# A chunked retention and gated-MLP kernel: one stretch of small products per chunk, a shorter weight conversion, another order

## The chip, the cores and the metric

The kernel runs on one core of a Trainium2 chip. TensorE (PE) multiplies into PSUM, with its weight loads shown apart (PEld); VectorE (DVE), ScalarE (ACT) and GpSimd (POOL) work on vectors; SyncE (SP) issues loads. The metric is the device time of one execution in microseconds (us), the median of several runs; smaller is better. The profile is one profiled execution, whose span runs from its first to its last instruction.

## The reference

Eight heads of linear attention with a decay, then a gate from a causal convolution of five taps, and two products with 512x512 weights. B = 4, S = 768, 8 heads of 64; the weights and taps come as float64.

```
gamma = 1.0 - 2.0 ** (-5.0 - np.arange(H))
for t in range(S):
    state = gamma * state + outer(k[:, :, t], v[:, :, t])
    y[:, :, t] = scale * (q[:, :, t] @ state)
x = y.transpose(0, 2, 1, 3).reshape(B, S, H * D)
gate = sigmoid(sum(conv_w[k] * xp[:, k:k + S] for k in range(5)))
out = (gate * (x @ w_val)) @ w_out
```

## The kernel before

The sequence is cut in 24 chunks of 128 tokens (g = 0 to 23), six per batch entry; chunks 4n to 4n+3 are the same tokens of the four entries and make unit n. A chunk's q, k, v (1 MB, tile `att`) come with one load on SP, five chunks deep. GpSimd multiplies v by its decay (`decay`, L251).

A chunk's attention is a series of small products, 64x64 in float32, each a quarter of the TensorE array; an fp32 product is two instructions in the profile. In each half of 64 tokens: `scores` (q times k, L261) into the left half of the tile `sy`; VectorE masks them into `u` (`mask`, L271); `y_scores` (u times v, L299) into the right half of `sy`; `state` adds k times v to the running state `z_ps` in PSUM (L283); ScalarE copies the state before each half (`snap`, L294); `y_state` adds that state times q (L299). VectorE scales y into `x` (`evac`, L344). On TensorE this is two blocks a chunk: `block_a` has y_scores and the first half's state, `block_b` the second half's state, y_state and, from chunk 6 on, the next chunk's scores. `block_b` comes after ScalarE's snapshot, with big products between the blocks.

A unit's MLP: for each of four column blocks m, `conv` (first tap on ScalarE, four on VectorE, L445, of which the planner may put two on TensorE, `pe_tap`, L454) and the sigmoid; `x` is split in a rounded part `xh` (ScalarE, L353) and a rest `xl` (GpSimd, L357); a value tile is 12 big products (`val`, L471), with which VectorE multiplies the gate (`gated`, L480); the result is split too (L487, L491). An output tile is 12 products (`outp`, L499) over all four blocks, copied by ScalarE (L509) and sent (L513). 24 value and 24 output tiles are 576 big products.

The float64 weights come as pairs of 32-bit words (`wst`) in eight tiles of 128x512. For each, VectorE runs five instructions (L388, L394, L400, L404, L417), ScalarE one (L409), GpSimd the sum (L413); then the split in two parts (L428, L432).

The order on every engine is written out by `plan`: each piece of work is a `Step` with a due time, an engine, a cost and the tiles that it reads and writes; the planner takes the step that can start first by its costs, the earliest due among equals. Due times stand in the constants at L534 to L543. An engine works strictly in that order.

Of the kernel before, what the change touches and what calls it, by code (L numbers as in the profile page):

```python
# [21 lines left out]
EARLY = 6  # L22
LB = 5
WB = 4
XB = 4
XS = 6
GV = 6
LATENCY, LANDING = 0.15, 1.8
PAGE, FETCH, CROWDED = 128, 3.4, 5.0
TINY = 2.0 ** -15 * (1.0 + 1.0 / 8.0)  # L30
LO, HI = slice(0, HALF), slice(HALF, P)

# [8 lines left out]
class Step:  # L41
    def __init__(self, due, engine, cost, reads, writes, fn, args):
        self.due, self.engine, self.cost, self.fn, self.args = due, engine, cost, fn, args
        self.reads, self.writes = reads, writes
        self.waits, self.then = set(), []
        self.next = []
        self.after = []
        self.lag = 0.0
        self.ready = 0.0
        self.words = 0  # L50
        self.other = None


def plan(steps):
# [31 lines left out]
    for ring in rings.values():  # L86
        for i, (k, s) in enumerate(ring):
            if i >= k.bufs:
                for b in users[ring[i - k.bufs][0]]:
                    wait(s, b)  # L90
            if i and s not in ring[i - 1][1].next:
                s.waits.add(ring[i - 1][1].index)
                ring[i - 1][1].next.append(s)
    clock, free = {}, {}
# [10 lines left out]
    order, words, paged = [], PAGE - 28, [0.0, 0.0]  # L105
    while any(free.values()):
        start, _, e = min(
            (max(clock[e], min(s.ready for s in f)), e, e) for e, f in free.items() if f
        )
        s = min((s for s in free[e] if s.ready <= start), key=lambda s: (s.engine != e, s.index))  # L110
        free[s.engine].remove(s)
        if s.other:
            free[s.other[0]].remove(s)
            if s.engine != e:
                s.engine, s.cost, s.fn = s.other
        order.append(s)
        clock[e] = start + s.cost
        if e == "PE" and s.words:

            left, now = s.words, start  # L120
            while left >= words:
                now += s.cost * words / s.words
                left -= words
                paged.append(now)
                slow = clock.get("DMA", 0.0) > now
                now, words = max(now, paged[-2] + (CROWDED if slow else FETCH)), PAGE
            words -= left
            clock[e] = max(clock[e], now + s.cost * left / s.words)
        for t in s.next:
            t.ready = max(t.ready, start)  # L130
            if t not in s.then:
                t.waits.discard(s.index)
                if not t.waits:
                    offer(t)
        for t in s.then:
            late = LANDING if e == "DMA" else 0.0 if t.engine == e else LATENCY
            t.ready = max(t.ready, clock[e] + late + s.lag)
            t.waits.discard(s.index)
            if not t.waits:
                offer(t)  # L140
    assert len(order) == len(steps)
# [4 lines left out]
def tile_retention_gated_mlp(  # L146
# [7 lines left out]
    eye: bass.AP,  # L154
    out: bass.AP,
):

# [13 lines left out]
    stage = ctx.enter_context(tc.tile_pool(name="stage", bufs=2))  # L194
    ps_y = ctx.enter_context(tc.tile_pool(name="ps_y", bufs=1, space=PSUM))
    ps_s = ctx.enter_context(tc.tile_pool(name="ps_s", bufs=1, space=PSUM))
# [3 lines left out]

    small_sb = const.tile([P, small.shape[1]], F32, name="small_sb")
    vd_sb = small_sb[:, 0:48].rearrange("p (c x) -> p c x", x=8)
    ra_sb = small_sb[:, 48:72].rearrange("p (c x) -> p c x", x=4)
    tri_sb = small_sb[:, 72:136]
    pos_sb = const.tile([2, P + 512], F32, name="pos_sb")
    cw_sb = const.tile([P, NPAIR, TAPS], F32, name="cw_sb")
    eye_sb = const.tile([P, P], F32, name="eye_sb")
    diag = const.tile([P, NPAIR, 2, P], F32, name="diag")
# [13 lines left out]
    def at(due, engine, cost, reads, writes, fn, *args):  # L222
        steps.append(Step(due, engine, cost, list(reads), list(writes), fn, args))

    parts, gates, gparts, xbufs = {}, {}, {}, {}
    chunks = [(b, c) for c in range(NCH) for b in range(B)]

# [17 lines left out]
    def sy_of(g):  # L245
        return sy1 if g < EARLY and g % 2 else sy0

# [6 lines left out]

    def scores(g):
        sy = sy_of(g)
        q, kT = halves(g, 0), halves(g, 1)
        for j in range(2):
            for s in range(2):
                for x, rows, cols in ((0, LO, LO), (1, HI, LO), (1, LO, HI), (0, HI, HI)):  # L260
# [6 lines left out]

    def mask(g):
        sy = sy_of(g)
        us[g] = mlp.tile([P, 2, 4, HALF], F32, name="u")  # L270
# [5 lines left out]
        )  # L276

# [13 lines left out]
    def snap(g, s):  # L291
        b, c = chunks[g]
        sn = mlp.tile([P, 2, 2, HALF], F32, name="snap", bufs=3)
# [3 lines left out]
    def y_mm(g, h, cols, j, s, lhsT, rhs, start):  # L297
        off = 256 + (2 * j + s) * HALF
        nc.tensor.matmul(  # L299
            sy_of(g)[cols, h, off:off + HALF], lhsT=lhsT, rhs=rhs,  # L300
# [9 lines left out]

    def y_state(g):
        b, c = chunks[g]
        q = halves(g, 0)
        for s in (1, 0):
            if c == 0 and s == 0:
                continue
# [4 lines left out]

    def first_pos():
        pos_ps.append(sy1[:, 0])
# [18 lines left out]
    def evac(g):  # L342
        b, c = chunks[g]
        nc.vector.tensor_tensor(  # L344
            xs[c][:, :, b, HALO:].rearrange("p (h j) t -> p h j t", h=2),
            sy_of(g)[:, :, 256:512].rearrange("p h (j t) -> p h j t", t=P),
# [4 lines left out]
    def round_x(n, ct):  # L351
        xh[n, ct] = mlp.tile([P, B, P], F32R, name="xh", bufs=XS)
        nc.scalar.copy(xh[n, ct], xs[n][:, ct, :, HALO:])  # L353

    def rest_x(n, ct):
        xl[n, ct] = mlp.tile([P, B, P], F32R, name="xl", bufs=XS)
        nc.gpsimd.tensor_tensor(  # L357
            xl[n, ct], xs[n][:, ct, :, HALO:], xh[n, ct].bitcast(F32), op=ALU.subtract
        )


    raws = {}

    def load_w(n):
        st = stage.tile([P, 512, 2], I32, name="wst", bufs=WB)
        src = w64[n // 4, n % 4].bitcast(I32).rearrange("p (n two) -> p n two", two=2)
        nc.sync.dma_start(out=st, in_=src)
        raws[n] = st

    cvt = {}  # L370

    def words(n):
        raw = raws[n]
        lo16 = raw.rearrange("p n two -> p (n two)").bitcast(U16).rearrange(
            "p (n four) -> p n four", four=4
        )[:, :, 1]
        return raw[:, :, 1], lo16

    def cv_bits(n):
        hi, _ = words(n)  # L380
        size = hi.shape[1]
        bits = ps_a.tile([P, 512], I32, name="acc")[:, 0:size]
        cvt[n] = (
            bits,
            stage.tile([P, size], I32, name="top"),
            stage.tile([P, size], F32, name="rest"),
        )
        nc.vector.tensor_scalar(  # L388
            bits, hi, 3, 0x3FFFFFFF, op0=ALU.logical_shift_left, op1=ALU.bitwise_and
        )  # L390

    def cv_top(n):
        bits, top, _ = cvt[n]
        nc.vector.scalar_tensor_tensor(  # L394
            top, words(n)[0], -0x40000000, bits, op0=ALU.bitwise_and, op1=ALU.bitwise_or
        )

    def cv_exp(n):
        bits, top, _ = cvt[n]
        nc.vector.tensor_scalar(bits, top, -0x800000, None, op0=ALU.bitwise_and)  # L400

    def cv_rest(n):
        bits, _, rest = cvt[n]
        nc.vector.scalar_tensor_tensor(  # L404
            rest, words(n)[1], 2.0 ** -36, bits.bitcast(F32), op0=ALU.mult, op1=ALU.mult
        )

    def cv_size(n):
        nc.scalar.activation(cvt[n][0].bitcast(F32), words(n)[0].bitcast(F32), AF.Abs)  # L409

    def cv_sum(n):
        _, top, rest = cvt[n]
        nc.gpsimd.tensor_tensor(rest, rest, top.bitcast(F32), op=ALU.add)  # L413

    def cv_flush(n):
        bits, _, rest = cvt[n]
        nc.vector.scalar_tensor_tensor(  # L417
            cw_sb.rearrange("p a k -> p (a k)") if n == "cw" else rest,
            bits.bitcast(F32), TINY, rest, op0=ALU.is_ge, op1=ALU.mult,
# [7 lines left out]
    def cv_round(n):  # L427
        nc.scalar.copy(parts_of(n)[0], cvt[n][2])  # L428

    def cv_low(n):  # L430
        h, l = parts_of(n)
        nc.gpsimd.tensor_tensor(l, cvt[n][2], h.bitcast(F32), op=ALU.subtract)  # L432
# [17 lines left out]
    def make_diag(m, i):  # L450
        nc.scalar.mul(diag[:, m, i], eye_sb, cw_sb[:, m, 1 + i:2 + i])

    def pe_tap(n, m, k):
        nc.tensor.matmul(  # L454
            accs[n, m], lhsT=diag[:, m, k - 1], rhs=xs[n][:, m, :, k:k + P],
            start=False, stop=True, skip_group_check=True,
        )

# [4 lines left out]
    def val(n, m, i):  # L463
# [3 lines left out]
        if i == 0:  # L467
# [6 lines left out]
            rhs=xx[n, ct].rearrange("p b t -> p (b t)"),  # L474
# [14 lines left out]
    def rest_gv(n, m):  # L489
        gvh, gvl = gvs[n, m]  # L490
        nc.gpsimd.tensor_tensor(gvl, gate.pop((n, m)), gvh.bitcast(F32), op=ALU.subtract)  # L491
# [23 lines left out]

    warm = nc.const_aps.tensor(0.0, (P, 1), F32).bitcast(BF16)[:, 0:1]

    def warm_up(i):

        dst = ps_a.tile([P, 512], F32, name="acc") if i < 2 else sy1[:, i % 2]  # L520
        nc.tensor.matmul(  # L521
            dst, lhsT=warm.broadcast_to([P, P]), rhs=warm.broadcast_to([P, 512]),
# [11 lines left out]
    MM = 0.232  # L534
    EARLY_AT = 3.46
    EARLY_STEP = 2.26
    LATE_AT = 29.71
    LATE_STEP = 6.0
    MLP_AT = 31.96
    MLP_STEP = 3.6  # L540
    SPLIT_LEAD = 5.44
    CONV_LEAD = 6.16
    W_AT = (9.3, 13.0, 15.6, 22.7, 36.8, 32.1, 37.6, 38.1)  # L543
# [3 lines left out]
    def load_at(due, g):  # L547
        loaded[g] = due
        a = [("att", g % LB, "qk"), ("att", g % LB, "vk")]
        if g == 0:  # L550
            at(due, "DMA", 3.2, [], a[0:1], load, g, slice(0, 2))
            at(due, "DMA", 1.6, [], a[1:2], load, g, slice(2, 4))
            at(due, "ACT", 0.4, [], ["small"], get, small_sb, small)
            at(due, "ACT", 0.4, [], ["pos"], get, pos_sb, pos)
# [277 lines left out]
```

## Time and profile before

| what | value |
|---|---|
| runs | 229.59, 229.29, 228.21 us; median 229.29 us |
| span of the profiled execution | 226.3 us (the page gives no other time for it) |
| busy: PE, DVE, ACT, POOL | 208.8, 140.0, 106.7, 105.9 us |

The page's slices show TensorE's share, the granted clock and the transfers in 40 equal parts of 5.66 us, in tenths:

```profile
PE   8666796797999999999999999999999999999993
DVE  0499858999999959377376329973339752911000
PEclk9857559999999999999999999999999999999999
DMA  6999979855145634564446524010111111111122
```

For ten slices the transfers are at their limit, VectorE fills up and TensorE has gaps; from the eleventh on TensorE is full to the end. Lines in the prediction have an engine, a line number and a tile, as in `PE mm L471`: a big product of a value tile.

### The profile page before, as it was taken

What the parts mean: (1) busy time and instruction counts of PE and PEld (TensorE: products, weight loads), DVE (VectorE), ACT (ScalarE), POOL (GpSimd) and SP (SyncE); (2) the same over time, 40 slices, a digit from 0 to 9 for tenths busy, and PEclk for the clock granted to TensorE, in tenths of its full rate; (3) what the DMA queues carried; (4) which work ended last, traced back from release to release, by engine and by line L of the source; (5) the groups of instructions that cost most, each with busy time, mean ns of one, the idle gap of its engine ahead of it and who ended that gap; (6) DMA issues with size and microseconds to landing.
All of it is one profiled execution on the core that took longest, in us unless ns stands there. A gap on an engine that the chain in (4) does not pass through costs nothing.

```text
span 226.3 us, 7941 instructions
## 1 busy us (share of the span) xinstructions
PE 208.8 (92%) x3551; PEld 162.8 (72%) x3551; DVE 140.0 (62%) x212; ACT 106.7 (47%) x218; POOL 105.9 (47%) x93
## 2 busy tenths in 40 slices
PE   8666796797999999999999999999999999999993
PEld 3365684665876787787777787777777888788883
DVE  0499858999999959377376329973339752911000
ACT  2373375455858346652472364541456437331421
POOL 0267889466999316824451644600526217220400
PEclk9857559999999999999999999999999999999999
DMA  6999979855145634564446524010111111111122
GB/s 205 421 414 416 410 271 363 305 212 184 30 167 191 211 123 181 185 226 133 151 197 234 186 77 175 38 49 5 47 49 46 46 46 49 46 46 46 46 93 96
DMA packets 8822, 36.32 MB, mean 161 GB/s; under 512 B 1106, under 2 KB 1618, under 8 KB 5844
## 3 DMA queue, kind: packets, MB, share of 16 engines
q1 hardware_dynamic: 4752, 29.36, 34.6%
q10 hardware_dynamic: 4036, 6.45, 7.6%
q8 instruction: 28, 0.46, 0.8%
q14 instruction: 6, 0.05, 0.1%
HBM read 29.52 MB, written 6.29 MB: 158 GB/s over the span
## 4 chain that ended last, share of the span: by engine, by line
PE 80%; DVE 10%; issue 4%; DMA 2%; POOL 1%; ACT 1%; ACTq 0%; POOLq 0%
PE mm L499 28%; PE mm L471 27%; PE sy L299 10%; PE z_ps L283 5%; PE sy L261 5%; PE sy L521 2%; DVE acc L445 2%; DMA out_dram<-o_sb 2%; DVE acc L400 1%; DVE x L344 1%; DVE rest L417 1%; DVE top L394 1%; POOL rest L413 1%; DVE u L271 1%; PE acc L454 1%
## 5 line engine op out<-in xcount | busy, mean ns | idle before, releaser
L445 DVE SCALAR_TENSOR_TENSOR acc<-x,cw_sb,acc 128x512 f32<-128x512 f32 x94 | 70.2, 753 | 19.3 <-ACT acc L443 17.4
L357 POOL TENSOR_TENSOR xl<-x,xh 128x512 fp32r<-128x512 f32 x24 | 30.5, 1293 | 39.8 <-PE mm L471 24.8
L491 POOL TENSOR_TENSOR gvl<-gate,gvh 128x512 fp32r<-128x512 f32 x24 | 30.8, 1294 | 28.4 <-ACT gvh L487 18.4
L499 PE MATMUL mm<-woh,gvl 128*128 128x512 f32 (+1 forms) x100 | 39.2, 392 | 0.0
L499 PE MATMUL mm<-wol,gvh 128*128 128x512 f32 (+1 forms) x100 | 39.2, 392 | 0.0
L499 PE MATMUL mm<-woh,gvh 128*128 128x512 f32 (+1 forms) x100 | 39.2, 392 | 0.0
L251 POOL TENSOR_TENSOR att<-att,small_sb 128x512 f32<-128x512 f32 x24 | 25.0, 1045 | 29.4 <-DMA att<-in_att_dram 29.3
L480 DVE TENSOR_TENSOR gate<-mm,gate 128x512 f32<-128x512 f32 x24 | 16.4, 687 | 22.5 <-PE mm L471 22.5
L509 ACT COPY o_sb<-mm 128x512 f32<-128x512 f32 (+1 forms) x25 | 14.2, 569 | 31.8 <-PE mm L499 30.2
L471 PE MATMUL mm<-xh,wvh 128*128 128x512 f32 x96 | 27.8, 406 | 0.1
L471 PE MATMUL mm<-xl,wvh 128*128 128x512 f32 x96 | 27.8, 402 | 0.0
L471 PE MATMUL mm<-xh,wvl 128*128 128x512 f32 x96 | 27.4, 400 | 0.0
L283 PE MATMUL z_ps<-att 64*64 64x64 f32 x704 | 22.2, 242 | 3.5 <-ACT snap L294 2.7
L299 PEld LDWEIGHTS sy<-u,att 64*64 64x64 f32 x768 | 16.1, 154 | 12.9 <-issue 6.8
L283 PEld LDWEIGHTS z_ps<-att 64*64 64x64 f32 x704 | 17.2, 151 | 10.2 <-ACT snap L294 6.2
L299 PE MATMUL sy<-u,att 64*64 64x64 f32 x768 | 19.2, 244 | 5.0 <-DVE u L271 3.1
L487 ACT CAST gvh<-gate 128x512 fp32r<-128x512 f32 x24 | 14.9, 620 | 18.3 <-PE mm L499 9.3
L461 ACT ACTIVATE gate<-acc 128x512 f32<-128x512 f32 x24 | 14.3, 596 | 18.7 <-POOL gvl L491 10.8
L344 DVE TENSOR_TENSOR x<-sy,dec 128x512 f32<-128x512 f32 x20 | 13.8, 689 | 14.8 <-PE sy L261 14.2
L294 ACT COPY snap<-z_ps 128x256 f32<-128x256 f32 x44 | 15.2, 372 | 15.7 <-PE z_ps L283 15.3
L499 PEld LDWEIGHTS mm<-wol,gvh 128*128 128x128 f32 x100 | 18.8, 188 | 4.1
L499 PEld LDWEIGHTS mm<-woh,gvh 128*128 128x128 f32 x100 | 18.8, 188 | 4.1
(46 smaller groups left out, 269.9 us busy)
## 6 DMA issues: line engine op xcount, KB each, us to landing
att<-in_att_dram SPq DMA_DIRECT2D x23, 1024.0 KB, 6.9
out_dram<-o_sb ACTq DMA_DIRECT2D x23, 256.0 KB, 2.0
wst<-in_w_dram SPq DMA_DIRECT2D x8, 512.0 KB, 7.4
att<-in_att_dram SPq DMA_DIRECT2D x2, 512.0 KB, 4.8
out_dram<-o_sb ACTq DMA_DIRECT2D x2, 128.0 KB, 1.9
small_sb<-in_small_dram ACTq DMA_DIRECT2D x1, 68.0 KB, 4.5
eye_sb<-in_eye_dram ACTq DMA_DIRECT2D x1, 64.0 KB, 9.2
cw_raw<-in_conv_w_dram ACTq DMA_DIRECT2D x1, 20.0 KB, 7.0
```

What stands on the lines that cost most here:

```text
L251: nc.gpsimd.tensor_tensor(v, v, vd_sb[:, c, :].unsqueeze(2).broadcast_to([P, 8, HALF]), op=ALU.mult)
L283: nc.tensor.matmul(z_ps[cols, x, b, j], lhsT=k[rows, x, j, s, :], rhs=v[rows, x, j, s, :], start=g == 0 and s == 0 and j == 0, stop=True, ...
L294: nc.scalar.copy(sn, z_ps[:, :, b])
L299: nc.tensor.matmul(sy_of(g)[cols, h, off:off + HALF], lhsT=lhsT, rhs=rhs, start=start, stop=True, skip_group_check=True,)
L344: nc.vector.tensor_tensor(xs[c][:, :, b, HALO:].rearrange("p (h j) t -> p h j t", h=2), sy_of(g)[:, :, 256:512].rearrange("p h (j t) -> p ...
L357: nc.gpsimd.tensor_tensor(xl[n, ct], xs[n][:, ct, :, HALO:], xh[n, ct].bitcast(F32), op=ALU.subtract)
L445: nc.vector.scalar_tensor_tensor(acc, x[:, :, k:k + P], cw_sb[:, m, k:k + 1], acc, op0=ALU.mult, op1=ALU.add,)
L471: nc.tensor.matmul(vps[n, m], lhsT=w[:, m, ct * P:(ct + 1) * P], rhs=xx[n, ct].rearrange("p b t -> p (b t)"), start=(i == 0), stop=(i == 3 ...
L480: nc.vector.tensor_tensor(gv, vps.pop((n, m)), gv, op=ALU.mult)
L487: nc.scalar.copy(gvs[n, m][0], gate[n, m])
L491: nc.gpsimd.tensor_tensor(gvl, gate.pop((n, m)), gvh.bitcast(F32), op=ALU.subtract)
L499: nc.tensor.matmul(ops[n, b, cs.start][:, 0:cs.stop - cs.start], lhsT=gg[:, b * P:(b + 1) * P], rhs=w[:, ct, cs], start=(i == 0), stop=(i ...
```

## The change

The small products. A chunk from 4 on has one stretch: `visit` (y_scores of g, second state half of g, first state half of g+1), then, in the planner held directly behind it, `rest_of_visit` (y_state of g, scores of g+1). Between them stands `turn`, a ScalarE copy of one column of `sy` on 64 partitions, which waits for products of `visit`, and for which those of `rest_of_visit` wait. The first four chunks read no state: their scores are taken over the whole 128 tokens (`first_scores`, `first_mask`, `first_y`, into a tile `ye` of their own), and chunk 4 opens with `head`.

The conversion. ScalarE scales the low word (`cv_up`), GpSimd adds it to the high word as an integer, and VectorE keeps three of its five instructions. Weights 0 to 7 are converted in the order of due times around the first chunks.

The order. Loads come as chunk 1, weight 0, chunks 2 and 3, weights 1 and 2, chunk 4, weight 3. The MLP's first value tile stands behind chunk 4's visit; `FIRST` and `REST` give the sequence of chunks (v), value tiles (V) and output tiles (O). `x` is split chunk by chunk, right behind its evacuation, into one tile a unit. The taps on TensorE, their diagonal matrices and the identity load are gone. The planner has a rank from the latest need of its successors, other costs, and a model of TensorE's stretches and instruction pages; only the order that it prints matters to the chip.

```diff
+    def first_mask(g):
+        us[g] = mlp.tile([P, 2, 6, HALF], F32, name="u").rearrange("p x (j k) t -> p x j k t", j=2)
+        for x in range(2):
+            nc.vector.tensor_tensor(
+                us[g][:, x],
+                sy[:, x, 0:384].rearrange("p (j k t) -> p j k t", j=2, t=HALF),
+                tri3_sb.unsqueeze(1).broadcast_to([P, 2, 3, HALF]),
+                op=ALU.mult,
+            )
...
+    def head(g):
+        scores(g)
+        state(g, 0)
+
+    def visit(g):
+        y_scores(g)
+        if chunks[g][1] < NCH - 1:
+            state(g, 1)
+        if g + 1 < NG:
+            state(g + 1, 0)
+
+    def turn(g):
+        nc.scalar.copy(turned[HI], sy[HI, :, 256:257])
+
+    def rest_of_visit(g):
+        y_state(g)
+        if g + 1 < NG:
+            scores(g + 1)
...
-    def cv_exp(n):
-        bits, top, _ = cvt[n]
-        nc.vector.tensor_scalar(bits, top, -0x800000, None, op0=ALU.bitwise_and)
-
-    def cv_rest(n):
-        bits, _, rest = cvt[n]
+    def cv_up(n):
+        lo16 = raws[n].rearrange("p n two -> p (n two)").bitcast(U16).rearrange(
+            "p (n four) -> p n four", four=4
+        )[:, :, 1]
+        nc.scalar.mul(cvt[n][2], lo16, 2.0 ** -13)
...
-        nc.gpsimd.tensor_tensor(rest, rest, top.bitcast(F32), op=ALU.add)
+        _, top, up = cvt[n]
+        nc.gpsimd.tensor_tensor(top, top, up, op=ALU.add)
...
-            if k <= 2:
-                steps[-1].other = ("PE", 1.05, pe_tap)
...
+    LOADS = (("a", 1), ("w", 0), ("a", 2), ("a", 3), ("w", 1), ("w", 2), ("a", 4), ("w", 3))
+    FIRST = "s0 y0 z0 s1 s2 y1 z1 y2 s3 z3 z2 y3 h4".split()
+    REST = (
+        "vvVVvVVvvOVVvvVOOOvVVVvOOOOvVVOvvO"
+        "VVVvOvOvVOvOOvvVOvvVVVOVVVOOVOOOOO"
+    )
...
+        step = at(t, "PE", 1.0, [u, vk] + ([("att", (g + 1) % LB, "vk")] if g + 1 < NG else []), [y, "z"], visit, g)
+        step.turn = at(t + 0.5, "ACT", (0.25, 0.2), [y], ["turn"], turn, g)
...
+        step.hold = at(t + 1.0, "PE", 1.0, reads, writes, rest_of_visit, g)
```

Three places of the new order. First TensorE at one chunk in the middle (chunk 10 before): y_scores and the first state half are the first two rows, the second block the three `z_ps`, `sy` rows further down.

```order
L299 MATMUL sy<-u,att 64x64 x16
L283 MATMUL z_ps<-att 64x64 x8
L471 MATMUL mm<-xh,wvh 128x512 x4
L471 MATMUL mm<-xh,wvl 128x512 x4
L283 MATMUL z_ps<-att 64x64 x8
L299 MATMUL sy<-att,snap 64x64 x16
L261 MATMUL sy<-att 64x64 x16
L471 MATMUL mm<-xl,wvh 128x512 x4
```

After (chunk 9), the same engine:

```order
L582 MATMUL mm<-xl,wvh 128x512 x3
L391 MATMUL sy<-u,att 64x64 x16
L375 MATMUL z_ps<-att 64x64 x16
L391 MATMUL sy<-att,snap 64x64 x16
L331 MATMUL sy<-att 64x64 x16
L582 MATMUL mm<-xh,wvh 128x512 x4
```

The 64 small products of a chunk now stand together; no big products are between them.

Second, TensorE where unit 0's last gating is needed: the value tile of unit 1 takes the PSUM bank that this gating frees. `mm_1043` (before) and `mm_1030` (after) are that value tile, `mm_1073` and `mm_1001` the first output tile. Before:

```order
L261 MATMUL sy_96<-att_616 64x64 x16
L471 MATMUL mm_1043<-xh_931,wvh_91 128x512
L471 MATMUL mm_1043<-xh_962,wvh_91 128x512
...
L471 MATMUL mm_1043<-xl_976,wvh_91 128x512
L499 MATMUL mm_1073<-woh_93,gvh_812 128x512
L499 MATMUL mm_1073<-wol_94,gvh_812 128x512
```

After:

```order
L331 MATMUL sy_95<-att_555 64x64 x16
L610 MATMUL mm_1001<-woh_92,gvh_767 128x512
L610 MATMUL mm_1001<-wol_93,gvh_767 128x512
...
L610 MATMUL mm_1001<-woh_92,gvl_996 128x512
L582 MATMUL mm_1030<-xh_577,wvh_90 128x512 x4
L610 MATMUL mm_1001<-woh_92,gvh_1032 128x512
```

Nine products of the output tile (those of three gated blocks) moved ahead of the value tile.

Third, ScalarE's first rows, which issue the small loads and load the sigmoid's table. Before:

```order
L239 DMA small_sb<-in_small_dram 128x136
L239 DMA pos_sb<-in_pos_dram 2x640
L239 DMA cw_raw<-in_conv_w_dram 128x40
L239 DMA eye_sb<-in_eye_dram 128x128
L528 ACT_TABLE_LOAD
L528 ACTIVATE sig<-const-float32-0.0 128x1
```

After:

```order
L311 DMA pos_sb<-in_pos_dram 2x640
L638 ACT_TABLE_LOAD
L638 ACTIVATE sig<-const-float32-0.0 128x1
L311 DMA small_sb<-in_small_dram 128x264
L311 DMA cw_raw<-in_conv_w_dram 128x40
```

The table load and the first sigmoid moved ahead of the loads of `small_sb` and `cw_raw`, the tap weights.

More of the change, by code (lines that the diff above doesn't have):

```diff
@@ L93, in plan @@
                 ring[i - 1][1].next.append(s)
+    left = [0] * len(steps)
+    before = [[] for _ in steps]
+    for s in steps:
+        for t in set(s.then) | set(s.next):
+            before[t.index].append(s)
+            left[s.index] += 1
+    ends = [s for s in steps if not left[s.index]]
+    for s in ends:
+        s.rank = s.due
+    while ends:
+        t = ends.pop()
+        for s in before[t.index]:
+            if s.engine == "PE" or not hasattr(s, "rank"):
+                s.rank = min(getattr(s, "rank", s.due if s.engine == "PE" else 1e9), 1e9)
+            lag = s.cost + SEEN.get(t.engine, 0.0) if t in s.then else 0.0
+            s.rank = min(s.rank, t.rank - lag) if s.engine != "DMA" else s.due
+            left[s.index] -= 1
+            if not left[s.index]:
+                ends.append(s)
     clock, free = {}, {}
@@ L104, in plan, with fetch, run_pe, offered @@
             offer(s)
[L105 to L128, printed above, removed]
+    order, landed = [], 0.0
+    pairs, left, arrives, kind = 0.0, float(FIRST_PAGE), 0.0, "big"
+    def fetch(now):
+        nonlocal left, arrives
+        now = max(now, arrives)
+        left += PAGE
+        arrives = now + (CROWDED if landed > now + 1.0 else FETCH)
+        return now
+    def run_pe(s, now):
+        nonlocal left, kind
+        slow = COLD if now < WARM_AT else 1.0
+        if s.small:
+            if kind == "big":
+                now += INTO
+            kind = "small"
+            todo, each = s.small, PAIR * slow
+        else:
+            if kind == "small":
+                now += OUT_OF
+            kind = "big"
+            todo, each = s.big, s.gap / max(1, s.big) * slow
+        while todo > left:
+            now += left * each
+            todo -= left
+            left = 0.0
+            now = fetch(now)
+        left -= todo
+        now += todo * each
+        return now, now + (0.21 if s.small else 0.17) * slow
+    held = None
+    def offered(e):
+        return free[e] if e != "PE" or held is None else [s for s in free[e] if s is held]
+    def done(s, end):
+        s.end, s.free = end, clock[s.engine]
         for t in s.next:
-            t.ready = max(t.ready, start)
+            t.ready = max(t.ready, s.start)
             if t not in s.then:
@@ L550, in load_at @@
         if g == 0:
[L551 to L554, printed above, removed]
-            at(due, "ACT", 0.4, [], ["cwraw"], get, cw_raw,
-               conv_w.bitcast(I32).rearrange("p (n two) -> p n two", two=2))
-            at(due, "ACT", 0.4, [], ["eye"], get, eye_sb, eye)
-            for s in steps[-4:]:
-                s.lag = 5.0
-        else:
-            at(due, "DMA", 2.6, [], a, load, g)
@@ L593, in attention @@
-        at(t + 0.7, "DVE", 0.62, [sc, "small"], [u], mask, g)
-        taken = [Slot("snap", 3) for _ in range(2)]
-        z = ("z", b)
-        if c > 0:
-            at(t + 0.9, "ACT", 0.38, [z], taken[0:1], snap, g, 0)
-        else:
-            taken = taken[1:]
-        at(t + 1.5, "PE", 1.05 * slow, [u, vk], [y, z], block_a, g)
-        steps[-1].words = 64
-        at(t + 2.7, "ACT", 0.38, [z], taken[-1:], snap, g, 1)
-        more, new = [], []
-        if ahead and g + 1 < NG:
-            scored[g + 1] = Slot("s%d" % bank, 1)
-            more, new = [("att", (g + 1) % LB, "qk")], [scored[g + 1]]
@@ L626, in convert @@
+        whole[c] = t + 2.0
     def convert(t, n):
         raw = wsts[n] if n != "cw" else "cwraw"
[L628 to L639 removed]
+        acc, top, up = Slot("acc", 2), Slot("top", 2), Slot("up", 2)
@@ L805, in _layout @@
         "pos": posr.astype(f),
-        "eye": np.eye(P, dtype=f),
     }
```

475 lines of the change are left out of this document (272 added, 203 removed).

## The prediction

> **What bounds the kernel now.** I read the 40 slices first, then the chain in order of time, then single stretches. The chain shows one engine, TensorE, without a gap from about 57 us on; before that it runs through VectorE, the weight loads and short waits. So the kernel has two parts with different limits, and the change is priced in each apart.
>
> ```profile
> span 226.3 us, 7941 instructions
> ...
> 60.77 2.53 PE mm L471 x10
> ...
> 100.33 0.62 PE sy L299 x32
> 100.96 0.23 PE z_ps L283 x16
> 101.19 2.06 PE mm L499 x8
> 103.25 0.39 PE z_ps L283 x16
> 103.64 0.47 PE sy L299 x32
> 104.11 0.47 PE sy L261 x32
> 104.58 1.13 PE mm L499 x4
> 105.70 2.33 PE mm L471 x10
> 108.03 0.62 PE sy L299 x32
> ...
> 172.27 2.80 PE mm L471 x12
> ...
> 222.42 0.27 PE L499 MATMUL mm<-woh,gvl 128*128 128x256 f32 x1
> ```
>
> Columns: start, length, engine, tile, line, count. A big product costs 2.80/12 = 0.2333 us. A small one (64x64, fp32) is two instructions in these rows; 32 of them take 0.47 us where nothing else is mixed in, 0.0147 each. From 100.33 to 108.03, 7.70 us, one chunk goes by: 22 big products (5.13), 128 small instructions (1.88), and 0.69 that is neither. The chunk's small work stands in two stretches, so each stretch costs 0.345 us for entering and leaving it: the first rows of a stretch read 0.62 instead of 0.47 and the big products behind it 2.06 instead of 1.87.
>
> I check this on the whole second part. At 60.77 TensorE starts the first value tile of unit 1; 528 of the 576 big products remain (123.2 us), 1,824 small instructions (26.8), 30 stretches (10.35) and one tap on TensorE (1.09, row below): 161.4 us, which ends at 222.2. The last product ends at 222.69. The sum carries to 0.5 us, and what follows the last product takes 226.3 - 222.7 = 3.6 us. The median of the runs, 229.29, is 3.0 us above this execution's span; I add that at the end.
>
> The first part is VectorE's.
>
> ```profile
> 8.80:60.30 51.50, 39.32 (x1118) 32.81 (x1122) 46.62 (x76) 28.84 (x66) 37.27 (x33) 0.80 0.78 305
> ...
> L445 DVE SCALAR_TENSOR_TENSOR acc<-x,cw_sb,acc 128x512 f32<-128x512 f32 x15 | 11.3, 753 | 0.3
> L271 DVE TENSOR_TENSOR u<-sy,small_sb 128x512 f32<-128x512 f32 x9 | 6.2, 686 | 1.3 <-PE sy L261 1.3
> L388 DVE TENSOR_SCALAR acc<-wst 128x512 int32<-128x512 int32 x8 | 5.5, 685 | 0.0
> L400 DVE TENSOR_SCALAR acc<-top 128x512 int32<-128x512 int32 x7 | 4.9, 695 | 0.2
> L404 DVE SCALAR_TENSOR_TENSOR rest<-wst,acc 128x512 f32<-128x512 uint16 x7 | 4.8, 687 | 0.2
> L394 DVE SCALAR_TENSOR_TENSOR top<-wst,acc 128x512 int32<-128x512 int32 x7 | 4.8, 682 | 0.1
> L417 DVE SCALAR_TENSOR_TENSOR rest<-acc,rest 128x512 f32<-128x512 f32 x6 | 4.1, 685 | 1.7 <-POOL rest L413 1.7
> ...
> 8.82 0.18 DVE L388 TENSOR_SCALAR acc<-cw_raw 128x20 int32<-128x20 int32 x1 [7.89 <-DMA cw_raw<-in_conv_w_dram]
> ...
> 59.01 1.28 DVE L480 TENSOR_TENSOR gate<-mm,gate 128x512 f32<-128x512 f32 x2
> ```
>
> The first row is the busy time of PE, PEld, DVE, ACT and POOL between VectorE's first real instruction and its fourth gating product: 46.62 of 51.50 us, 4.9 idle. The fourth gating (end 60.29) closes unit 0, and right after it the long TensorE part starts.
>
> **The change part by part.** Second part first. After the change TensorE meets the fourth gating in this order: nine products of the first output tile, then the value tile of unit 1. Behind that point stand 519 big products (121.1 us), 1,808 small instructions (26.6) and 15 stretches instead of 30 (5.2): 152.9 us against 161.4. The 8.5 us are 5.2 for the stretches, 2.1 for the nine products that moved ahead of the wait, 0.2 for 16 small instructions, and the tap:
>
> ```profile
> 68.91 1.09 PE acc L454 x2
> ```
>
> The tap that goes to VectorE costs it 0.75 and is hidden there, since VectorE is busy 69 of 106 us in the row of the next fence. If that cover goes, gates come late and TensorE stands before the next value tile. The snapshots of the state for the first four chunks, the diagonal matrices and the eye load lie in ScalarE's and the queue's free time before 60 us; I cost their removal at nothing.
>
> The new wait is the one-column copy on ScalarE (`turn`), in the middle of each stretch: TensorE's state reads wait for it, and it waits for the products before it.
>
> ```profile
> 63.00:169.00 106.00, 105.84 (x2117) 81.60 (x2116) 68.77 (x101) 52.73 (x109) 49.43 (x42) 1.00 0.38 137
> ...
> 65.80 0.28 PE z_ps L283 x14
> ...
> 66.15 0.66 ACT snap L294 x2
> ...
> 66.85 0.46 PE z_ps L283 x16
> ...
> 4.26 0.20 ACT L528 ACTIVATE sig<-const-float32-0.0 128x1 f32<-128x1 f32 x1
> ```
>
> TensorE's end (66.08) reaches ScalarE in 0.07 us, ScalarE's end (66.81) reaches TensorE in 0.04; a copy of one column is nearest to the 0.20 row. In a visit the score products are through at 0.62 us, so the copy ends at about 0.9 and its release stands at 0.95; meanwhile TensorE still has 32 state instructions and is ready at 0.15 + 64 x 0.0147 = 1.1. With a free ScalarE the wait is nothing. ScalarE is busy half of the time here (52.73 of 106) with instructions of 0.37 to 0.69 us; one begun just before holds the copy up by at most 0.5 us more than the slack. Half of 15 visits at some 0.27 is 2.0 us; the ends are 0 and 7.5. I take 2.0, nearer to the low end, because a handover of this kind (TensorE idle from 66.08 to 66.85) is paid only once in this part of the trace.
>
> TensorE's instructions also have to arrive.
>
> ```profile
> q8 instruction: 28, 0.46, 0.8%
> ...
> 19.81 0.65 PE L261 MATMUL sy<-att 64*64 64x64 f32 x30
> ...
> 22.67 0.21 PE L261 MATMUL sy<-att 64*64 64x64 f32 x1 [2.22 <-issue]
> ...
> 27.97 0.36 PE L283 MATMUL z_ps<-att 64*64 64x64 f32 x1 [0.83 <-issue]
> ...
> 78.63 0.62 PE sy L299 x32
> ...
> 82.40 0.47 PE sy L261 x32
> ```
>
> 28 packets of 16 KB carry some 7,100 instructions of TensorE, 254 each, 127 with their weight loads. In the loading phase it stops in the middle of a run of products, at 22.67 and, 128 instructions and 5.3 us later, at 27.97. Counted on in steps of 127.5, two turns of a page in the quiet part lie only 4.0 us apart (78.6 and 82.6, between the last two rows), without a wait. A visit uses a whole page in 2.2 us. Where n big products stand between two visits, 128 + n instructions take 2.22 + 0.233n us: 3.85 for n = 7 (twice), 4.3 for 9, 5.0 for 12 (twice), 5.7 for 15. At 4.0 us a page only the two sevens lose, 0.4 each: 0.8 us, my value. At 5.3 us a page it is 1.8, 1.4, 0.8 and 0.2: 6.7 in all, the upper end; none is the lower.
> The Trainium skill, page "Runtime: NRT & Kernel Launch", section "Instruction fetch mechanics", says that pages of 256 instructions are fetched while the one before executes and that crossing one is mostly hidden. By it this term would be 0 and the sum 0.8 us less. The size of a page agrees; the 2.22 us row does not, so the trace decides.
>
> Now the first part: when does the fourth gating end? From VectorE's work up to it go L400 and L404 (9.7 us) and two tiny ones (0.35). All eight weights are now converted ahead of it, which adds one L394 and two L417 (2.05) and the L388 that had just begun (0.6). The first four masks become two instructions of 128x384 each: between 0.18 us for 20 elements and 0.69 for 512 this is 0.55, so +0.41 a chunk, 1.65. One mask, one evacuation (0.69 each) and one tap (0.75) more stand ahead of it. Net -3.6; neighbours overlap (the groups add up to 50.6 for 46.6 busy), so -3.3.
>
> ```profile
> 1.74 0.36 ACTq L239 DMA_DIRECT2D cw_raw<-in_conv_w_dram  x1
> 2.97 1.28 ACT L528 ACT_TABLE_LOAD   x1 [2.97 <-issue]
> ...
> cw_raw<-in_conv_w_dram ACTq DMA_DIRECT2D x1, 20.0 KB, 7.0
> ```
>
> Against it, the table load (1.28) and the first sigmoid (0.20) now stand on ScalarE's queue ahead of the loads of the small table and of the tap weights. cw_raw is issued at about 3.2 instead of 1.74, and with its 7.0 us of landing VectorE starts 1.4 late. Of the 4.9 us idle the waits for the GpSimd sum (1.7) mostly go, as the chain of a conversion has two links less; the waits for chunks stay, because the load order brings them at the pace of the queue. I take 3.6 idle; the ends are 1 and 7. The fourth gating ends at 60.3 - 3.3 + 1.4 - 1.3 = 57.1.
>
> Sum: 57.1 + 152.9 + 2.0 + 0.8 + 3.6 = 216.4 us of span against 226.3; with 3.0 around it, 219.4.
>
> **Rivals.** *The start does not shorten*: the chunks and instruction pages set the pace, VectorE idles 7 us. The fourth gating is then at 60.5 and the time 222.8. For it speaks the full queue (0.78 busy up to 60 us); against it, that VectorE was 91% busy. *The start runs without loss* and ScalarE is always free: gating at 54.5, no waits, 214.0. *Pages*: 5.3 us each all along, 225.3; with the slow start as well 228.7, no change. *The copy decides, slower*: ScalarE works strictly in order, and the copy stands behind instructions that wait themselves.
>
> ```profile
> ACT gate L461 <- POOL gvl L491: 10.8, 8, 4.3
> ```
>
> Such waits are 1.35 us in the mean (10.8 over 8). If every visit met one, 15 x 1.35 = 20 us come instead of 2.0: 237.6, slower. It decides from 0.8 us a visit on, where the gain of 12 us without the copy is used up. Against it: before had a wait of the same kind (state products behind a snapshot) fifteen times in this part, and TensorE was still 105.84 of 106 us busy.
>
> **How the numbers follow.** A measurement of this kernel tells about 1% (2.3 us) from no change. Chances: my forecast with 216 to 222 us 0.46; the start without loss (213 to 216) 0.20; the slow start (222 to 224.5) 0.13; pages (about 225) 0.08; pages with a slow start, no change, 0.08; the copy, slower, 0.05. Faster by over 1% is 0.46 + 0.20 + 0.13 + 0.08 = 0.87, within 1% 0.08, slower 0.05. The predicted time is the forecast's, 219.4. From 213.5 to 225.5 the first four cases are held but for a few hundredths, about 0.83.
>
> **What would show it.** In the new chain a chunk should be one run of small products of about 2.2 us between big ones, with no ScalarE row inside; a `turned` row inside it, or a wait of PE for ACT L441 of over 3 us in all, shows my 2.0 wrong. The fourth L591 row on VectorE should end near 57 and TensorE be full from there; its first row on the tap weights (L509 of the changed code) near 10.2. TensorE's waits on issue behind that point should be under 1 us. What would make the prediction wrong: VectorE reaching the fourth gating later than 60, ScalarE late in most visits, or value tiles waiting for gates after 60 us, since each has four taps on VectorE now (3.7 us a tile with its gating against 2.8 on TensorE).

## The result, and the profile after

The changed kernel takes 220.73 us (median of 4 runs, 220.42 to 222.05), the kernel before 229.3 beside it. The ratio is 0.965, interval 0.961 to 0.968. The forecast was 219.4, range 213.5 to 225.5.

The page of the changed kernel, first the span and the slices, then TensorE's instruction queue:

```profile
span 218.8 us, 7821 instructions
...
PE   8578649995999999999999999999999999999993
...
DVE  0177979798999803994023499622799378920000
...
PEclk9965979998799999999999999999999999999998
...
q8 instruction: 27, 0.44, 0.9%
```

TensorE is full from about 60 us on, as before, but VectorE has more gaps up to there, and TensorE's clock dips once more, to 8 and 7 in the two slices from 49 to 60 us. The two parts of the prediction, in the view by stretches (busy time of PE, PEld, DVE, ACT, POOL), and TensorE's last product:

```profile
10.23:60.54 50.31, 40.40 (x1065) 33.83 (x1065) 42.20 (x71) 33.65 (x73) 44.12 (x39) 0.83 0.79 309
...
60.54:215.41 154.87, 154.41 (x2341) 125.12 (x2339) 86.84 (x130) 72.64 (x156) 60.83 (x50) 1.00 0.32 114
...
215.13 0.28 PE L610 MATMUL mm<-woh,gvl 128*128 128x256 f32 x1
```

The fourth gating ends at 60.54 (before: 60.29). Behind it TensorE needs 154.87 us to its last product's end at 215.41; before it was 222.69 - 60.29 = 162.4. So all of the gain in the span, 7.5 us, came behind the fourth gating, and the first part gave none. The median time fell by 8.6 us: in the runs on record a span of 226.3 us goes with a time of about 228.2, so the profiled execution of the kernel before was some 1 us faster than its median. One chunk there, in the view in order of time:

```profile
106.67 0.69 PE L391 MATMUL sy<-u,att 64*64 64x64 f32 x32
107.19 0.65 PE L375 MATMUL z_ps<-att 64*64 64x64 f32 x32
107.43 0.15 ACT L441 COPY turned<-sy 64x2 f32<-64x2 f32 x1 [1.94 <-DMA out_dram<-o_sb]
107.65 0.68 PE L391 MATMUL sy<-att,snap 64*64 64x64 f32 x32
108.16 0.65 PE L331 MATMUL sy<-att 64*64 64x64 f32 x32
```

It is one run of small products, the copy takes 0.155 us, and TensorE goes on without a gap. In the waits behind 60.6 us (us in all, times, longest) the copy is small:

```profile
PEld sy L391 <- ACT turned L441: 1.0, 4, 0.4
...
PE sy L391 <- ACT turned L441: 0.3, 1, 0.3
```

The first part is another picture. VectorE's rows that waited, and its fourth gating:

```profile
10.23 0.18 DVE L509 TENSOR_SCALAR acc<-cw_raw 128x20 int32<-128x20 int32 x1 [9.30 <-DMA cw_raw<-in_conv_w_dram]
...
16.50 1.02 DVE L363 TENSOR_TENSOR u<-sy,small_sb 128x384 f32<-128x384 f32 x2 [1.08 <-PE sy L344]
...
33.31 0.69 DVE L353 TENSOR_TENSOR u<-sy,small_sb 128x512 f32<-128x512 f32 x1 [1.74 <-PE sy L331]
...
43.92 0.69 DVE L536 SCALAR_TENSOR_TENSOR top<-acc,top 128x512 f32<-128x512 f32 x1 [1.72 <-ACT acc L527]
...
50.35 0.76 DVE L565 SCALAR_TENSOR_TENSOR acc<-x,cw_sb,acc 128x512 f32<-128x512 f32 x1 [0.76 <-ACT acc L563]
...
59.86 0.68 DVE L591 TENSOR_TENSOR gate<-mm,gate 128x512 f32<-128x512 f32 x1
```

VectorE worked 42.20 of 50.31 us: 4.4 less than before. But it started 1.4 us later (10.23 for 8.80) and idled 8.1 instead of 4.9, which uses the 4.4 up. By what ended the waits, 5.0 of the 8.1 us were for TensorE's products of chunks (2.3 before), 1.7 for the size on ScalarE (L527) and 0.8 for its first tap (L563). TensorE and ScalarE in the same time:

```profile
24.09 0.50 PE L375 MATMUL z_ps<-att 64*64 64x64 f32 x17 [1.06 <-issue]
...
30.16 0.37 PE L391 MATMUL sy<-u,att 64*64 64x64 f32 x2 [2.75 <-issue]
...
52.65 0.69 PE L391 MATMUL sy<-att,snap 64*64 64x64 f32 x32 [2.28 <-ACT turned L441]
...
42.46 0.15 ACT L441 COPY turned<-sy 64x2 f32<-64x2 f32 x1 [1.41 <-PE sy L391]
...
43.16 0.65 ACT L527 ACTIVATE acc<-wst 128x512 f32<-128x512 f32 x1
```

TensorE stops in the middle of chunk four's products for instructions (2.75 us; VectorE's 1.74 at 33.31 follows from it). At chunk six ScalarE stands 1.41 us for the copy, with the next cast and size behind it, and VectorE's 1.72 at 43.92 waits for that size. At chunk seven the copy is late for TensorE.

### The profile page after: what moved, and what is told of

The parts are those of the page before. It is cut to its first block, busy times and chain, and to the rows that moved or that the text cites. A ratio compares the mean times of both kernels' runs of the same rounds, so it can differ in the third digit from the quotient of the medians.

```text
span 218.8 us, 7821 instructions
## 1 busy us (share of the span) xinstructions
PE 202.8 (93%) x3483; PEld 162.3 (74%) x3483; DVE 129.2 (59%) x200; ACT 109.7 (50%) x235; POOL 106.3 (49%) x93
## 4 chain that ended last, share of the span: by engine, by line
PE 81%; DMA 8%; DVE 3%; issue 3%; ACT 2%; SPq 1%; POOL 0%; ACTq 0%; DVEq 0%
PE mm L610 30%; PE mm L582 30%; PE sy L391 11%; DMA att<-in_att_dram 7%; PE z_ps L375 4%; PE sy L331 4%; PE ye L408 1%; DMA out_dram<-o_sb 1%; SPq L308 1%; DVE top L515 1%; DVE u L353 1%; ACT acc L563 1%; PE sy L344 1%; ACT acc L527 1%; DVE acc L509 1%
## 5 line engine op out<-in xcount | busy, mean ns | idle before, releaser
L602 POOL TENSOR_TENSOR gvl<-gate,gvh 128x512 fp32r<-128x512 f32 x24 | 30.9, 1290 | 43.3 <-ACT gvh L598 30.8
L610 PE MATMUL mm<-woh,gvl 128*128 128x512 f32 (+1 forms) x100 | 37.7, 394 | 0.0
L610 PE MATMUL mm<-woh,gvh 128*128 128x512 f32 (+1 forms) x100 | 37.3, 389 | 0.0
L610 PE MATMUL mm<-wol,gvh 128*128 128x512 f32 (+1 forms) x100 | 37.0, 386 | 0.0
L582 PE MATMUL mm<-xl,wvh 128*128 128x512 f32 x96 | 35.5, 408 | 0.0
L582 PE MATMUL mm<-xh,wvh 128*128 128x512 f32 x96 | 32.8, 402 | 0.0
L353 DVE TENSOR_TENSOR u<-sy,small_sb 128x512 f32<-128x512 f32 x20 | 13.7, 686 | 21.2 <-PE sy L331 21.2
L610 PEld LDWEIGHTS mm<-woh,gvl 128*128 128x128 f32 x100 | 18.7, 188 | 4.5 <-POOL gvl L602 0.2
L582 PEld LDWEIGHTS mm<-xl,wvh 128*128 128x128 f32 x96 | 18.4, 193 | 4.4
L582 PEld LDWEIGHTS mm<-xh,wvl 128*128 128x128 f32 x96 | 17.8, 188 | 4.7 <-issue 0.5
L582 PEld LDWEIGHTS mm<-xh,wvh 128*128 128x128 f32 x96 | 17.5, 188 | 4.6 <-DVE gate L591 0.4
```

The lines of the kernel that those rows point to most:

```text
L353: nc.vector.tensor_tensor(us[g], sy[:, :, 0:256].rearrange("p x (a t) -> p x a t", t=HALF), tri_sb.unsqueeze(1).unsqueeze(1).broadcast_to( ...
L582: nc.tensor.matmul(vps[n, m], lhsT=w[:, m, ct * P:(ct + 1) * P], rhs=xx[n][:, ct].rearrange("p b t -> p (b t)"), start=(i == 0), stop=(i = ...
L602: engine.tensor_tensor(gvl, gate.pop((n, m)), gvh.bitcast(F32), op=ALU.subtract)
L610: nc.tensor.matmul(ops[n, b, cs.start][:, 0:cs.stop - cs.start], lhsT=gg[:, b * P:(b + 1) * P], rhs=w[:, ct, cs], start=(i == 0), stop=(i ...
```

## The experiments

Theories: (A) entering and leaving stretches of small products is what the second part gained; (B) VectorE's work sets the first part; (C) chunks and TensorE's instruction pages set it; (D) the copy in ScalarE's strict order gave VectorE's saved work back. Each run is compared with runs of the kernel before on its chip, whose median there was 228.4 to 228.8 us; differences from the changed kernel of about 1 us are therefore read from the spans, of the profiled execution (218.8 in the changed kernel) or as the median of a kernel's runs (218.7). To read the traces I use TensorE's *lost time*: the time at which a chunk's products on `u` start, less 0.2333 us for every big and 0.0147 for every small instruction ahead of it in the program.

| lost by TensorE, us, at chunk | 4 | 8 | 11 | 19 | last product |
|---|---|---|---|---|---|
| before | 21.4 | 32.3 | 35.5 | 41.0 | 44.4 |
| changed | 20.4 | 30.8 | 32.5 | 35.4 | 38.5 |
| two_stretches | 19.6 | 32.0 | 35.1 | 42.1 | 45.6 |
| after_old_conversion | 25.2 | 38.4 | 41.6 | 44.6 | 47.7 |
| before_new_conversion | 22.0 | 34.0 | 38.1 | 43.6 | 47.0 |
| long_copy | 20.7 | 32.5 | 35.4 | 41.8 | 46.9 |
| copy_six_later | 20.4 | 30.0 | 31.4 | 34.4 | 37.5 |

**Two stretches again (A).**

```diff
-        if e == "PE":
-            held = s.hold
```

> The changed kernel, but big products may again stand between the two halves of a chunk's small products: 38 stretches instead of 20, the same instructions. If entering and leaving a stretch is what costs (0.345 us each, from the trace of before), 18 more of them cost 6.2 us; less the 1.3 us that TensorE waits for the copy behind 60 us in the changed kernel: about 225.5 us, and TensorE's busy time is higher by about 4 to 6 us. If the gain came from elsewhere (the shorter conversion, the MLP's earlier start), the time stays within 1 us of 220.7.

228.48 us, ratio 1.000 (0.997 to 1.004): 7.75 more than the changed kernel, as much as the change had gained. The chain around one chunk:

```profile
96.18 0.62 PE sy L389 x32
96.81 0.47 PE z_ps L373 x32
97.27 0.42 PE mm L580
97.70 0.62 PE sy L389 x32
98.32 0.47 PE sy L329 x32
98.79 6.26 PE mm L608 x26
```

One big product between the halves takes 0.42 us there, and the second half begins with a 0.62 again. Lost time from chunk 11 to the end is 10.5 us against 6.0; a chunk costs 0.7 in most places and 0.36 in the changed kernel. The span is 7.1 us longer (225.9). The fourth gating ends 1.4 us later, at 61.90, and from there to TensorE's last product it takes 160.55 us, 5.7 more. Of these, 1.5 are other waits at two places (1.1 and 1.8 us lost at a chunk instead of 0.7), and 0.7 are three big products that stand ahead of the gating in the changed kernel. The remaining 3.5 us are what the expectation says for 14 stretches behind the gating: 4.8 less 1.3 for the copy. So A holds at its forecast price; that the whole gain went is in part chance. The other part of the gain, the products moved ahead of the gating and the tap, is mostly not undone in this run: the kernel before takes 162.4 us there.

**The conversion: undone in the changed kernel, done alone in the one before (B or C).** The old five VectorE steps in place of the new ones, and the reverse:

```diff
-        at(t + 0.01, "ACT", cost("ACT"), [raw], [up], cv_up, n)
+        at(t + 0.02, "DVE", cost("DVE"), [top], [acc], cv_exp, n)
+        at(t + 0.03, "DVE", cost("DVE"), [raw, acc], [rest], cv_rest, n)
```

> The changed kernel with the old conversion of seven instructions before the rounding, five of them on VectorE: 16 more VectorE instructions of 0.6 us ahead of the fourth gating, 9.7 us. If VectorE's work sets the end of the first part, the fourth gating comes 9 to 10 us later (near 70) and the time is near 230. If chunks, TensorE's instruction pages and the copy on ScalarE set it, the 8.1 us that VectorE idles there take up most of it: fourth gating at 62 to 65, time 222 to 225.

> The kernel before with the short conversion alone, nothing else: 7 x 2 VectorE instructions (9.7 us) less ahead of the fourth gating at 60.3. If VectorE's work sets the first part, the fourth gating comes at 51 to 53 and the time is near 221; if the chunks and TensorE's pages set it, 2 to 4 us earlier at most, 225 to 227. The second part stays at 161 to 162 us in both.

The first: 229.31 us, ratio 1.003 (1.001 to 1.006), fourth gating at 69.16. So in the new order the short conversion is worth 8.6 us, near the 9.7 of its instructions: B. The second: 231.5 us, ratio 1.012 (1.008 to 1.017), slower than before, fourth gating at 63.08. From the fourth gating to TensorE's last product it takes 155.4 us in the first and 162.2 in the second: the second part goes with the order, not with the conversion. VectorE up to its fourth gating in both, same columns as above:

```profile
10.74:69.16 58.42, 42.54 (x1062) 36.98 (x1063) 52.20 (x89) 28.00 (x59) 45.84 (x40) 0.74 0.69 265
```

```profile
8.42:63.08 54.66, 41.41 (x1140) 34.05 (x1141) 39.98 (x64) 34.79 (x78) 39.11 (x35) 0.78 0.75 289
```

In the old order VectorE's work fell by 6.6 us and its idle time rose from 4.9 to 14.7. Of the 14.7, 6.4 us are waits for TensorE's products of chunks (2.3 before), 3.8 for GpSimd's sum (1.7 before) and 1.7 for the size on ScalarE. That the old due times brought them about is likely but was not tried. Neither theory had a slower kernel. New order and short conversion together are worth what neither is alone.

**VectorE's start (B or C).** The planner is told another landing time for the tap weights.

```diff
-        steps[-1].cost = 5.0 + n
+        steps[-1].cost = 5.0 + n if n < 2 else 10.0
```

> The changed kernel, planned as if the tap weights landed three us later, so that VectorE's first instruction is the mask of the first chunk and not the conversion of the tap weights, for which it stood until 10.23. If VectorE's start is part of what sets the end, the first mask is near 8.2, two us earlier, and the time falls by 1.5 to 2 us, to about 219. If the chunks set the pace up to 26 us (VectorE idles 3.2 us between 13 and 26 for TensorE's products on chunks two to four), the two us are given back by then and the time stays at 220.7, within 0.8.

225.55 us, ratio 0.987 (0.985 to 0.989): 4.8 slower than the changed kernel, against both expectations (span 223.7). The plan also put the first evacuation ahead of the conversions, and VectorE stood for it:

```profile
8.57 1.02 DVE L363 TENSOR_TENSOR u<-sy,small_sb 128x384 f32<-128x384 f32 x2 [7.63 <-PE sy L344]
13.76 0.69 DVE L471 TENSOR_TENSOR x<-ye,base 128x512 f32<-128x512 f32 x1 [4.17 <-PE ye L408]
```

With 7.5 instead of 10.0 only the mask changes places:

> The changed kernel with one exchange on VectorE: the first mask stands ahead of the first instruction on the tap weights, all other instructions of VectorE and TensorE in their old order from the sixth on. The mask then starts near 8.6 instead of 10.32, and the evacuation of the first chunk no longer stands ahead of the conversions. If what VectorE loses in the first part goes through to the end (the long conversion cost 8.6 us, the early evacuation 4.8), 1 to 1.7 us earlier: near 219.3. If the waits for chunks and pages behind it take the gain up, 220.7 within 0.5.

221.22 us, ratio 0.969 (0.967 to 0.972): no gain to speak of. In the profile (span 218.5) the fourth gating ends at 60.16, 0.4 earlier than in the changed kernel. The mask starts 1.65 us earlier, but at 43.92 and at 50.35 VectorE waits at the very times of the changed kernel, and TensorE stops once more for instructions:

```profile
8.67 1.02 DVE L363 TENSOR_TENSOR u<-sy,small_sb 128x384 f32<-128x384 f32 x2 [7.74 <-DMA small_sb<-in_small_dram]
...
43.92 0.69 DVE L536 SCALAR_TENSOR_TENSOR top<-acc,top 128x512 f32<-128x512 f32 x1 [1.71 <-ACT acc L527]
...
36.46 0.40 PE L391 MATMUL sy<-u,att 64*64 64x64 f32 x11 [1.32 <-issue]
```

**Instruction pages (C).** Three runs: the last four weights loaded behind chunks seven and eight; half a page more of instructions at the start (the warm-up in pieces); half a page less (half of the first chunks' state products left out).

```diff
+            steps[-1].after = [s for s in steps if s.engine == "DMA" and s.args[0] in (7, 8) and s.fn is load]
```

```diff
-            ye[:, i % 2], lhsT=warm.broadcast_to([P, P]), rhs=warm.broadcast_to([P, 512]),
+                ye[:, i % 2, cols], lhsT=warm.broadcast_to([P, P]), rhs=warm.broadcast_to([P, 85]),
```

```diff
         state(g, 0)
-        state(g, 1)
```

> The changed kernel, but the loads of weights four to seven stand behind the loads of chunks seven and eight in the queue, so that fewer bytes are outstanding from 21 us on, when TensorE's next page of instructions is fetched. If outstanding loads make that page slow (6.1 us from 24.1 to 30.2, against 3.4 between two turns near 122 us with the engines as busy), TensorE's stop of 2.75 us in chunk four falls below 1.5 and the time by 0.5 to 2 us. If the page is slow for another reason, the stop stays within 0.5 of 2.75. The planner sets a somewhat different order of value products behind 33 us; a later conversion of the last weights could cost up to 2 us.

> The changed kernel with 78 warm-up products of 85 columns instead of 13 of 512: the same columns in the same time ahead of the first chunk, the order on all engines unchanged, but TensorE's program is 65 products (130 instructions, half a page) longer at its beginning. If the supply of TensorE's instructions (a page every 6.1 us from 24 to 36 us, the same in four kernels) is what took up VectorE's saved work, chunks three to five come up to 3 us later and the time is 2 to 3 us longer, near 223. If pages don't set the pace, 220.7 within 0.6.

> The changed kernel without the second half of the state products of the first four chunks (64 products of 64x64 in all are left out of the computation), the order of all else unchanged. By the supply of instructions half a page less is needed ahead of chunk five: chunk five's visit starts at 33 instead of 35.9 and the time falls by 1.5 to 3 us, to 218 to 219; the 64 products themselves are 0.9 us of TensorE at 0.0147 each, in a part where it waits for other things. If pages don't set the pace, 220.7 within 0.8.

Late weights: 225.89 us, ratio 0.990 (0.987 to 0.992). The stop in chunk four stayed, 2.48 us, the page came 5.8 us after the one before instead of 6.1; the late conversions then held up the gates (TensorE waits 3.62 us for one at 62.16). More instructions: 221.82, ratio 0.973 (0.967 to 0.979); the spans of its four runs have a median of 219.8, 1.1 above the changed kernel's and between the two expectations. In its profile (span 219.2) the fourth gating ends at 60.31, no later than in the changed kernel (60.54), so the first part did not become longer. Fewer: 221.72, ratio 0.970 (0.966 to 0.974), span 219.3, fourth gating at 60.97, not shorter at all. TensorE's stops in the two:

```profile
25.08 0.50 PE L331 MATMUL sy<-att 64*64 64x64 f32 x18 [1.12 <-issue]
...
31.26 0.27 PE L391 MATMUL sy<-att,snap 64*64 64x64 f32 x2 [1.56 <-issue]
...
37.30 0.40 PE L391 MATMUL sy<-att,snap 64*64 64x64 f32 x13 [1.08 <-issue]
```

```profile
30.92 0.37 PE L391 MATMUL sy<-att,snap 64*64 64x64 f32 x2 [1.42 <-issue]
...
32.18 2.07 PE L581 MATMUL mm<-xh,wvh 128*128 128x512 f32 x4
```

The stops move with the program, 6.1 us apart, but chunk six starts at 41.2 and 41.7 us, in the changed kernel at 41.3. Shorter stops were replaced by other waits, and with fewer instructions the clock was low behind the stop (0.50 from 32 to 34 us, four big products in 2.07 us). This fits pages as one of several limits of about the same height before 41 us; pages alone do not set the end. The other half of C, the chunks, was not tested by taking their waits away: they are 5.0 of VectorE's 8.1 us.

**The plan's price of a page.**

```diff
-FIRST_PAGE, PAGE, FETCH, CROWDED = 94, 127.5, 3.5, 5.5
+FIRST_PAGE, PAGE, FETCH, CROWDED = 94, 127.5, 3.5, 6.1
```

> The changed kernel, planned with 6.1 us for a page in the loading phase (as measured) instead of 5.5; the same work and loads, the order of ScalarE, VectorE and value products shifted by up to some instructions between 30 and 60 us. If the waits of 2.3 us for the copy at chunk seven and 1.7 us of VectorE at 43.9 come from a plan that runs ahead of the chip, they shrink and the time falls by 1 to 2 us; if not, 220.7 within 0.8.

222.62 us, ratio 0.976 (0.974 to 0.979), some 2 us more than the changed kernel; the fourth gating ends at 62.06, and the wait for the copy at chunk seven grew to 2.88. A truer price made no better order.

**The copy's length.** It copies 256 columns of both banks instead of one.

```diff
-        nc.scalar.copy(turned[HI], sy[HI, :, 256:257])
+        nc.scalar.copy(turned[HI], sy[HI, :, 256:512])
```

> The changed kernel with a one-column copy that takes 256 columns of both banks: some 0.55 us instead of 0.155. In the trace the copy ends 0.05 to 0.1 us before TensorE's weight loads are through with the state products. If the copy's length is what stands between the halves of a stretch, TensorE waits 0.3 to 0.35 us at each of the 16 visits behind 60 us and the time is 5 to 7 us longer, 226 to 228, the stretches 0.7 instead of 0.35 us beside their products. If the wait has slack, under 1 us longer.

229.1 us, ratio 1.004 (1.001 to 1.006): 8.4 more than the changed kernel, above the 5 to 7 expected. The copies of this run:

```profile
L441 ACT COPY turned<-sy 64x512 f32<-64x512 f32 x20 | 11.6, 580 | 23.3 <-PE sy L391 19.4
```

The copy takes 0.580 us, 0.425 more, and a chunk between 11 and 19 loses 0.80 us instead of 0.36: all of it is paid. The handover has no slack left. The fourth gating comes 2.1 us later (62.62), and the second part takes 161.2 us, 6.3 more.

**The copy's place on ScalarE (D).** The list that the planner returns, with one step moved, then a second one:

```diff
+        copy = todo.pop(find(turn, 6))
+        todo.insert(find(cv_size, 5) + 1, copy)
```

```diff
+        first = todo.pop(find(tap, 0, 3, 0))
+        todo.insert(find(turn, 7) + 1, first)
```

> The changed kernel with one instruction of ScalarE moved: the copy of chunk six stands behind the next cast and the next size instead of ahead of them; nothing else differs. In the changed kernel ScalarE stood 1.41 us for this copy (to 42.46), the size came at 43.16 and VectorE idled 1.72 us for it. If a copy that waits in ScalarE's strict order is what gave VectorE's saved work back, this idle falls below 0.5 us, and since VectorE idles only 1.05 us more up to its fourth gating, the time falls by 0.7 to 1.7 us, to 219 to 220. If TensorE's own stops set the time, 220.7 within 0.4.

> The same, and on ScalarE the first tap of gate three of unit 0 (which waits for VectorE) stands behind the copy of chunk seven instead of ahead of it. TensorE's stop of 2.28 us before the state reads of chunk seven falls to 0.7 or less. If VectorE's work sets the fourth gating, this gives nothing beyond the run with the one move (within 0.4 us, or worse by 0.3 for the later tap); if TensorE's stop is what counts, 1 to 2.5 us more, near 217 to 218.

One move: 219.97 us, ratio 0.964 (0.960 to 0.968). VectorE's idle time at that place falls to 0.91 (the next to be late is GpSimd's sum), and the fourth gating ends at 59.52, 1.0 us earlier; so does the span, 217.8.

```profile
43.10 0.69 DVE L536 SCALAR_TENSOR_TENSOR top<-acc,top 128x512 f32<-128x512 f32 x1 [0.91 <-POOL top L531]
...
58.84 0.68 DVE L591 TENSOR_TENSOR gate<-mm,gate 128x512 f32<-128x512 f32 x1
```

The times' intervals overlap with those of the changed kernel, so the 1.0 us stand on the trace; the median span of the runs (218.0) is 0.7 below the changed kernel's. Both moves: 221.26 us, ratio 0.969 (0.964 to 0.973), span 218.0, fourth gating at 59.78. The median span of its runs, 219.2, is 1.2 above that with one move, more than the 0.4 expected, and the profiled execution does not show why. TensorE's stop of 2.28 us is gone, and it waits as long for VectorE instead:

```profile
55.34 0.69 PE L391 MATMUL sy<-u,att 64*64 64x64 f32 x32 [2.34 <-DVE x L471]
```

So from 44 to 60 us VectorE sets the pace, and TensorE's stop there cost nothing. D holds for the part that was tried, 0.7 to 1.0 us, and not for the rest of VectorE's idle time.

## Why the prediction was right, and where it was not

- *Stretches*: right. The 0.345 us per stretch came back as 0.36 per chunk, and putting 14 stretches back behind the fourth gating cost 3.5 us net of the copy, as forecast.
- *Behind the fourth gating*: forecast 152.9 + 2.0 + 0.8 = 155.7, measured 154.87. The copy cost 1.3 us there instead of 2.0, most of it in the last four chunks, which have fewer state products to cover it. The mechanism (a wait by chance behind ScalarE's other instructions) was wrong: such a wait hardly came, but the cover is so exact that 0.425 us more of copying cost 0.44 a chunk. Pages cost nothing seen instead of 0.8. Of the 154.87, some 0.7 are not traced to a wait.
- *First part*: this step failed. Forecast for the fourth gating 57.1, measured 60.54. VectorE's start was right (10.23 for 10.2), but not by the reason given: the tap weights were issued at 1.77, while the table load ran (1.30 to 2.58), and took 8.4 us to land. That the two errors cancelled is luck. VectorE's work was right too, 42.2 us for 43.3. The wrong term is "I take 3.6 idle; the ends are 1 and 7": it was 8.1. GpSimd's sum waits went as forecast. The waits for chunks, which the forecast let stay, rose from 2.3 to 5.0 us; stops for instruction pages and the pace of the first chunks are in them, and no run took them away. ScalarE's size and first tap, at nothing in the forecast, took 2.5; ahead of the size stood the copy, in strict order and planned too early, and moving it brought the gating 1.0 us forward. The copy had been priced for TensorE in the second part only, not for what is queued behind it on ScalarE while VectorE is the bound.
- *Tail and surroundings*: 3.4 us behind the last product (forecast 3.6), and 1.9 from the span to the median instead of 3.0. The 3.0 compared the median with the span of another execution; in most runs on record the time is 1.8 to 2.2 us above that run's own span. So 219.4 + 3.4 - 0.8 - 0.2 - 1.1 = 220.7. The sum came within 1.3 us because three smaller errors took back 2.1 of the 3.4; that is luck.
- *Rivals*: "the start does not shorten" was right in its number (60.5), and in part in its cause: it let VectorE idle 7 us for chunks and pages, and the chunks took 5.0 of 8.1. It gave 222.8 because it kept the forecast's copy, pages and surroundings, all of which came out smaller. The copy did not decide against the change.

The Trainium skill, page "Runtime: NRT & Kernel Launch", section "Instruction fetch mechanics", has page crossings mostly hidden. Behind 60 us this trace agrees, against my 0.8; before 40 us it does not, with stops of 1.06 and 2.75 us.

What stays open: which of chunks, pages and clock holds chunk six at 41.2 to 41.7 us in six of the kernels. No run removed the 3.2 us that VectorE idles between 13 and 26 us.

## What to carry to other kernels

Where small products interrupt large ones, count how often TensorE changes between them, not only the products. A wait added to an engine that works in strict order has to be priced twice: for who waits for it, and for what stands behind it on that engine in the part where another engine is the bound. Work taken off the busiest engine need not come back as time: here the same conversion was worth 8.6 us in one order and less than nothing in another.

## What was not expected of the hardware

TensorE's clock fell to half behind stops shorter than 3 us, and not always at once. Windows of the changed kernel (granted clock: the third number from the end):

```profile
30.00:32.00 2.00, 1.84 (x69) 1.83 (x71) 1.57 (x3) 0.59 (x3) 2.00 (x2) 0.50 1.01 418
...
52.00:54.00 2.00, 1.35 (x65) 1.23 (x65) 1.97 (x4) 1.84 (x5) 2.00 (x2) 0.88 0.00 0
54.00:56.00 2.00, 2.00 (x8) 1.16 (x12) 2.00 (x4) 0.91 (x2) 2.00 (x3) 0.50 0.68 242
```

Behind the stop of 2.75 us (to 30.16) it is 0.50 at once; behind that of 2.28 (to 52.65) it is 0.50 only from 54 on. The Trainium skill, page "TensorE: Matmul & The Clock Gate", section "Part 1: The HAM clock gate (the "warmup" mystery)", gives half rate after an idle window of about 3.4 us and tells that the window runs freely; the half rate agrees, and the stops here were shorter than the window.

The packets of TensorE's instruction pages (16 KB each) stand in the trace. In the changed kernel they start at 21.49, 27.56 and 34.02 us, 6.1 and 6.5 apart, while loads kept the DMA share at 1.0. With the last weights queued later, the page in chunk four came little sooner (5.8), but the next one only 3.7 us behind it (27.03 and 30.77), at the same share. Two loads of chunks were outstanding then; at 34.02 in the changed kernel it was four loads. So the share alone does not explain the slow pages; the loads queued may, and that was not settled. The 3.4 us near 122 us, which an expectation sets beside them, came from counting products in steps of 127.5; the packets there start at 117.62, 122.76 and 127.42, and no two are 3.4 apart.
